# Whole turns of a cosine as int32 from ScalarE, in a planned kernel of attention and two gated layers

## The chip, the cores and the metric

One core of a Trainium2 chip runs the whole program. The metric is the device time of one execution in microseconds, the median over the runs. TensorE multiplies matrices, VectorE, ScalarE and GpSimd work on tiles in SBUF (VectorE and ScalarE also on the banks of PSUM that TensorE writes), and SyncE issues nearly all transfers. In the views PE is TensorE's matmul, PEld its load of weights, DVE is VectorE, ACT ScalarE, POOL GpSimd and SP SyncE.

## What is computed

```python
def _moe_ref(x, w_in, w_out):
    h = x @ w_in
    g = h * np.clip(h + 3.0, 0.0, 6.0) / 6.0
    return g @ w_out

def _moe2_ref(x, w_in, w_out):
    h = x @ w_in
    g = h * np.cos(h)
    return g @ w_out

def reference(q, k, v, moe, moe2):
    a = _attn_ref(q, k, v)           # (2, 8, 768, 64): local window and block summaries
    x = a.transpose(0, 2, 1, 3).reshape(1536, 512)
    return _moe2_ref(_moe_ref(x, *moe), *moe2)
```

Both layers take 1536 tokens of 512 features to 2048 and back; the weights arrive as float64 and are read as pairs of 32-bit words.

## The kernel before, in words

The program has three stages: attention, layer 1 (the clipped gate) and layer 2 (the cosine gate). Every matrix factor is held as two parts, a rounded one (hi) and the rest (lo), and a product is three matmuls, hi by hi, hi by lo and lo by hi. `unpack` (L693 to L709) rebuilds a float from each pair of words of a weight: a ScalarE step (L696) and two VectorE steps (L700, L704). `parts` then makes the two halves of a weight tile wi or wo: a copy (L445 on ScalarE, L447 on GpSimd) and a subtraction (L452, VectorE or GpSimd).

The tokens form three blocks of 512, the 2048 features 16 chunks of 128 in four groups. In layer 2 each group has two *stretches*, where two chunks of the first two blocks are computed together by a scheme with seven products in place of eight (`unit`, L957; `pairs`, L723, prepares sums of weights at L733). Its intermediate sums o and s are made on VectorE from bank t (L1002). The third block's chunks are computed singly (`g1`, L754, matmuls at L766 to L768). Second matmuls (`g2`, L823, matmuls at L842) fill in between, and their results are added to part or pc on VectorE (L883). PSUM has eight banks: two each named acc, h and s, one t and one o.

Behind each first matmul comes `post` (L772 to L823), which makes g and its two parts out of a bank h (or t, o, s). In layer 1 that is one ScalarE step into a tile n and one VectorE step into a tile r. In layer 2 the cosine is computed by taking off whole turns:

```python
act(ACTF.Identity, n, h, ..., scale=1.0 / (2.0 * math.pi), bias=bias[:, 1:2])   # + MAGIC
n = n - MAGIC                       # L810, GpSimd or VectorE
stt(-C1, r, n, h, ...)              # r = h - C1 n, first step, L802
stt(-C2, r, n, r, ...)              # r = r - C2 n, second step, L802
act(ACTF.Abs, r, r, ...)
act(ACTF.Sin, r, r, ..., scale=-1.0, bias=bias[:, 2:3])
r = r * h                           # L817
```

MAGIC is 1.5 times 2 to the 23, so that adding it in float32 rounds to whole numbers. Then come the copy of r into g (L445 or L447) and the subtraction r - g (L452). The bank is free once L817 has read it. All ScalarE steps of `post` stand at L798, all `scalar_tensor_tensor` steps at L802.

The order of all instructions is written by a planner in the program. `Plan.op` collects operations with their candidate engines, costs and priorities; `order` plays them through on a model of the engines and emits each where that model puts it. An operation marked `port=True` counts as excluding GpSimd while VectorE runs it. A table T holds offsets of priorities, loads of engines and numbers of buffers, and NUDGES a list of seeds that disturb priorities. A change of a cost, a mark or the tables therefore moves rows on every engine and in SyncE's queue of loads.

Of the kernel before, what the change touches and what calls it, by code (L numbers as in the profile page):

```python
# [12 lines left out]
F32 = mybir.dt.float32  # L13
F32R = mybir.dt.float32r
U32 = mybir.dt.uint32
ACTF = mybir.ActivationFunctionType
ALU = mybir.AluOpType
AX = mybir.AxisListType
# [22 lines left out]
AW = QD + 2 * (NS - 1)  # L41
SP = S + 2 * WIN
NEG = -8.0e9
MAGIC = 1.5 * 2.0 ** 23
C1 = 6.28125
C2 = 2.0 * math.pi - 6.28125

# [16 lines left out]
def consts():  # L64
# [11 lines left out]


T = dict(
    A0=-16.558, AS=2.479, mask=-41.168, kp=-24.799, lk=-15.792, lq=-45.051, lv=4.367, wl=4.037, wc=-16.709,
    g0=37.025, gi=15.494, pp=74.729, fill=0.951, DVE=1.408, POOL=0.57, d0=0.9, warm=9, tail=1, lagq=1, nraw=3,  # L80
    ncf=2, n=5, w1=5, n2=1, g2=5, w2=3, f2=1, ne=3, npt=2, nz=3, u0=10.0, us=-1.723, vpe=27.388, lvt=-27.618,
    avg=-15.727,
)
NUDGES = (
    301030, 301046, 301214, 301262, 301298, 301299, 301311, 301317, 301338, 301363, 301389, 301404, 301405,
    301511, 301663, 301665, 301951, 302350, 302504, 302970, 303048, 303239, 303835, 304073, 304314, 304762,
    304806, 306020, 401406, 404014, 1004772,
)


# [37 lines left out]
class Plan:  # L128
# [10 lines left out]
    def op(self, engs, fn, prio, r=(), w=(), take=(), port=False, mode=0):  # L139
        o = Op()  # L140
        o.engs, o.fn, o.prio, o.port, o.mode, o.seq = engs, fn, prio, port, mode, len(self.ops)
        o.wait, o.after, o.ready, o.takes = 0, [], 0.0, list(take)
        o.start = o.eng = None
        o.took = False
        bufs = {id(x): x for x in take}
        before = set()
        for key in r:
            before.add(self.writer[key])
        for key in w:
            if key in self.writer:  # L150
                before.add(self.writer[key])
            before.update(self.readers.get(key, ()))
        for key in r:
            self.readers.setdefault(key, []).append(o)
        for key in w:
            self.writer[key] = o
            self.readers[key] = []
        for key in (*r, *w):
            x = key[0] if isinstance(key, tuple) else key
            if isinstance(x, Buf):  # L160
                bufs[id(x)] = x
        o.uses = list(bufs.values())
        for x in o.uses:
            x.uses += 1
        for key in r:
            x = key[0] if isinstance(key, tuple) else key
            if isinstance(x, Buf) and x.cls.bank:
                for a in self.readers[key]:
                    if a is not o and not (len(engs) == 1 and list(a.engs) == list(engs)):
                        before.add(a)  # L170
        before.discard(o)
        for x in before:
            x.after.append(o)
        o.wait = len(before)
        self.ops.append(o)
        return o
# [217 lines left out]
def body(ctx: ExitStack, tc: tile.TileContext, q, k, v, vf, w_in1, w_out1, w_in2, w_out2, ident_d, mask_d, avg_d, out):  # L394
    nc = tc.nc
    w_in = (w_in1.bitcast(U32), w_in2.bitcast(U32))
    w_out = (w_out1.bitcast(U32), w_out2.bitcast(U32))
    cp = ctx.enter_context(tc.tile_pool(name="cp", bufs=1))
    pp = ctx.enter_context(tc.tile_pool(name="pp", bufs=1, space=bass.MemoryType.PSUM))
# [3 lines left out]
    def slots(name, n, shape, dtype=F32, fifo=True, pool=cp, later=0):  # L403
        return Slots(lambda i, pool=pool: pool.tile(shape, dtype, name=f"{name}{i}"), n, later, fifo, pool is pp)

    mask = ap.tile([P, 3, CE], F32, name="mask")
    bias = cp.tile([P, 4], F32, name="bias")
# [5 lines left out]
    avg = ap.tile([P, AW + QD], F32, name="avg")  # L413
# [9 lines left out]
    ident = ap.tile([P, P], F32, name="ident")  # L423
    c_raw = slots("raw", T["nraw"], [P, DM, 2], U32)
    c_cu = slots("cu", 2, [P, DM])
# [15 lines left out]
    eng = {"DVE": nc.vector, "POOL": nc.gpsimd}  # L441

    def copy(e, out, in_, scale=1.0):
        if e == "ACT":
            nc.scalar.activation(out=out, in_=in_, func=ACTF.Copy, scale=scale)  # L445
        elif e == "POOL" or scale != 1.0:
            eng[e].tensor_scalar(out=out, in0=in_, scalar1=scale, scalar2=0.0, op0=ALU.mult, op1=ALU.add)  # L447
        else:
            nc.vector.tensor_copy(out, in_)

    def sub(e, out, in0, in1):
        eng[e].tensor_tensor(out=out, in0=in0, in1=in1.bitcast(F32), op=ALU.subtract)  # L452
# [6 lines left out]
    for x in c_vs.tiles:  # L459
        nc.gpsimd.memset(x, 0.0)  # L460
    nc.vector.memset(bias[:, 0:1], 0.5)
    nc.vector.memset(bias[:, 1:2], MAGIC)
    nc.vector.memset(bias[:, 2:3], 0.5 * math.pi)
    pl = Plan()
    op = pl.op
    pl.second = [c_cf, c_wi, c_g, c_n, c_r, c_p2, c_sx]
# [149 lines left out]
    def soft(h, sp, c0, e_, sm, prio):  # L616
        for i in range(HT):
            t = HT * h + i
            mk = mask[:, 0 if t == 0 else (2 if t == TB - 1 else 1), :]
            for o in range(2):  # L620
# [11 lines left out]
                    lambda e, x=x: nc.scalar.activation(  # L632
                        out=e_.t[:, x, :], in_=e_.t[:, x, :], func=ACTF.Exp, scale=-1.0,
                        bias=sm.t[:, x:x + 1], accum_out=sm.t[:, N4 + x:N4 + x + 1],
# [21 lines left out]

    A0, AS = T["A0"], T["AS"]
    load_consts()
# [7 lines left out]
    for b, h, ps in units:  # L666
        pr = A0 + AS * HT * y
        if h == 0:
# [23 lines left out]
    def unpack(src, prio, f, key, take):  # L692
# [3 lines left out]
           lambda e: nc.scalar.activation(  # L696
               out=u.t, in_=raw.t.bitcast(F32)[:, :, 1], func=ACTF.Prelu, scale=2.0 ** -112, alpha=2.0 ** 32),
           prio, r=[raw], w=[u], take=[u])
        op({"DVE": 0.34},
           lambda e: eng[e].tensor_scalar(  # L700
               out=f().bitcast(U32), in0=raw.t[:, :, 0], scalar1=2.0 ** -29, scalar2=7.0, op0=ALU.mult, op1=ALU.min),
           prio, r=[raw], w=[key], take=take, port=True)
        op({"DVE": 0.602},
           lambda e: nc.vector.scalar_tensor_tensor(  # L704
               out=f().bitcast(U32), in0=u.t.bitcast(U32), scalar=3, in1=f().bitcast(U32),
               op0=ALU.logical_shift_left, op1=ALU.bitwise_or),
# [33 lines left out]
    IT = 5.2  # L740
    G0 = A0 + AS * HT * NP + T["g0"]

# [32 lines left out]
    def post(it, hb, pr):  # L775
        L, N = it[0], it[5] - it[4]
        nb, rb, gb = Buf(c_n), Buf(c_r), Buf(c_g)

        def t(fixed, per):
            return fixed + per * N / TOK  # L780

        def h():
            return hb.t[:, 0:N]

        def n():
            return nb.row[:, 0:N]

        def r():
            return rb.row[:, 0:N]

        def hi():
            return gb.t[:, 0, 0:N]

        def lo():
            return gb.t[:, 1, 0:N]

        def act(func, out, in_, pr, fixed, rd, wr, take=(), **kw):
            op({"ACT": t(fixed, 0.43)}, lambda e: nc.scalar.activation(out=out(), in_=in_(), func=func, **kw), pr,  # L798
               r=rd, w=wr, take=take)

        def stt(s, out, a, b, o0, o1, rd, take=()):
            op({"DVE": t(0.056, 0.542)}, lambda e: nc.vector.scalar_tensor_tensor(  # L802
                out=out(), in0=a(), scalar=s, in1=b(), op0=o0, op1=o1), pr, r=rd, w=[rb], take=take)

        if L == 0:
            act(ACTF.Relu, n, h, pr, 0.146, [hb], [nb], [nb], scale=1.0 / 6.0, bias=bias[:, 0:1])
            stt(1.0, r, n, h, ALU.min, ALU.mult, [nb, hb], [rb])
        else:
            act(ACTF.Identity, n, h, pr, 0.146, [hb], [nb], [nb], scale=1.0 / (2.0 * math.pi), bias=bias[:, 1:2])
            op({"POOL": t(0.12, 0.463), "DVE": t(0.07, 0.265)}, lambda e: eng[e].tensor_scalar(  # L810
                out=n(), in0=n(), scalar1=1.0, scalar2=-MAGIC, op0=ALU.mult, op1=ALU.add), pr, w=[nb],
                port=True)
            stt(-C1, r, n, h, ALU.mult, ALU.add, [nb, hb], [rb])
            stt(-C2, r, n, r, ALU.mult, ALU.add, [nb])
            act(ACTF.Abs, r, r, pr, 0.11, [], [rb])
            act(ACTF.Sin, r, r, pr, 0.2, [], [rb], scale=-1.0, bias=bias[:, 2:3])
            op({"DVE": t(0.056, 0.542)}, lambda e: nc.vector.tensor_tensor(out=r(), in0=r(), in1=h(), op=ALU.mult),  # L817
               pr, r=[hb], w=[rb])
        op({"ACT": t(0.09, 0.435), "POOL": t(0.12, 0.463)}, lambda e: copy(e, hi(), r()), pr, r=[rb], w=[(gb, 0)],
           take=[gb])  # L820
        op({"DVE": t(0.07, 0.54), "POOL": t(0.125, 1.13)}, lambda e: sub(e, lo(), r(), hi()), pr,
           r=[rb, (gb, 0)], w=[(gb, 1)], port=True)
        return gb  # L823
# [85 lines left out]
    n = 0  # L909
# [7 lines left out]
    for j in range(NBLK):  # L917
        for x, y in ((0, TOK // 2), (TOK // 2, TOK)) if j == 0 else ((0, TOK),):
# [4 lines left out]
            for c in range(GS):  # L923
                pr = vt(n1 + c * d)
# [9 lines left out]
    pr = vt(T["u0"] - T["us"])  # L934
# [158 lines left out]
```

## Time and profile before

| | |
|---|---|
| median of 3 runs | 615.54 us (614.97 to 617.27) |
| the profiled execution | 616.4 us, of which the span of its trace is 614.5 |
| TensorE busy | 575.4 us, 94% of the span |
| VectorE busy | 486.8 us, 79% |
| GpSimd busy | 419.8 us, 68% |
| ScalarE busy | 314.0 us, 51% |
| mean granted TensorE clock | 0.992 of 2.4 GHz |

Busy time counts an instruction from its start to its end, and so contains what it waits for another engine in between. A row for a group of instructions gives the count, the busy time and the mean, then the idle time of the engine just ahead of them and what ended it. A clock of 1.00 is 2.4 GHz, of 0.50 is 1.2 GHz. A table by stage gives the busy time of each engine in a stretch of the span.

### The profile page before, as it was taken

The numbers are of one execution on the slowest core, as the hardware profiler recorded it, in microseconds if no ns is written. First come the engines' busy times: TensorE is split into PE (matmuls) and PEld (weight loads), VectorE is DVE, ScalarE is ACT, GpSimd is POOL, SyncE is SP. The second block draws the span as 40 slices with busy tenths as digits, with TensorE's granted clock in tenths as the row PEclk, the third lists the DMA queues.
The fourth block names the chain that finished last, engine by engine and source line by source line (L and its number), as shares of the span: only waits on it lengthen the run. The fifth ranks groups of instructions, "written<-read, shape, count | busy, mean of one in ns | idle before, by whom it ended". The sixth has DMA issues, their size and how long they took to land. (4 is left out here: it accounts for less than half of the span.)

```text
span 614.5 us, 9208 instructions
## 1 busy us (share of the span) xinstructions
PE 575.4 (94%) x3308; PEld 465.7 (76%) x3308; DVE 486.8 (79%) x807; ACT 314.0 (51%) x657; POOL 419.8 (68%) x417
## 2 busy tenths in 40 slices
PE   5868999999999999999999899999898999989997
PEld 4657988877788888888886577877786787867786
DVE  3599877998888379836989989975998689986962
ACT  2799877456433233223345666564543546445430
POOL 2579755999785458645989867956677668946540
PEclk9999999999999999999999999998999999989999
DMA  9999820013224004400330203220114003200122
GB/s 224 279 297 275 243 70 2 1 35 105 80 99 162 1 2 129 146 0 1 103 103 0 69 1 103 74 99 0 69 34 141 32 1 103 69 0 0 40 76 92
DMA packets 28910, 51.62 MB, mean 84 GB/s; under 512 B 14529, under 2 KB 17985, under 8 KB 28865
## 3 DMA queue, kind: packets, MB, share of 16 engines
q1 hardware_dynamic: 28720, 50.97, 27.1%
q8 instruction: 26, 0.43, 0.3%
q14 instruction: 20, 0.16, 0.1%
q10 hardware_dynamic: 144, 0.07, 0.0%
HBM read 47.88 MB, written 3.15 MB: 83 GB/s over the span
## 5 line engine op out<-in xcount | busy, mean ns | idle before, releaser
L452 POOL TENSOR_TENSOR g<-r,g 128x512 fp32r<-128x512 f32 (+1 forms) x78 | 108.9, 1397 | 5.3 <-ACT g L445 1.3
L447 POOL TENSOR_SCALAR g<-r 128x512 fp32r<-128x512 f32 (+1 forms) x57 | 39.8, 698 | 72.1 <-DVE r L802 48.7
L842 PE MATMUL acc<-g,wo 128*128 128x512 f32 (+1 forms) x384 | 87.7, 366 | 1.3 <-DVE g L452 1.3
L696 ACT ACTIVATE cu<-raw 128x512 f32<-128x512 f32 x64 | 43.1, 674 | 78.2 <-DVE cf L704 61.4
L842 PEld LDWEIGHTS acc<-g,wo 128*128 128x128 f32 x384 | 66.2, 189 | 14.3 <-DVE g L452 2.1
L842 PE MATMUL acc<-wo,g 128*128 128x512 f32 x288 | 73.7, 390 | 0.6 <-DVE pc L883 0.6
L842 PE MATMUL s<-wo,g 128*128 128x512 f32 x288 | 72.9, 394 | 0.0
L842 PEld LDWEIGHTS s<-wo,g 128*128 128x128 f32 x288 | 55.1, 191 | 12.0 <-DVE pc L883 0.4
L842 PEld LDWEIGHTS acc<-wo,g 128*128 128x128 f32 x288 | 54.0, 188 | 12.6 <-DVE pc L883 1.1
L704 DVE SCALAR_TENSOR_TENSOR cf<-cu,cf 128x512 uint32<-128x512 uint32 x64 | 62.0, 979 | 0.6
L842 PE MATMUL s<-g,wo 128*128 128x512 f32 x240 | 59.0, 389 | 0.0
L452 POOL TENSOR_TENSOR wi<-cf,wi 128x512 fp32r<-128x512 f32 x37 | 57.0, 1544 | 1.4
L810 POOL TENSOR_SCALAR n<-n 128x512 f32<-128x512 f32 x40 | 31.9, 798 | 37.3 <-ACT n L798 37.3
L842 PEld LDWEIGHTS s<-g,wo 128*128 128x128 f32 x240 | 45.1, 188 | 9.4
L700 DVE TENSOR_SCALAR cf<-raw 128x512 uint32<-128x512 uint32 x64 | 49.7, 795 | 2.4 <-POOL wo L452 1.5
L994 PE MATMUL t<-sx,wi 128*128 128x512 f32 x168 | 45.8, 408 | 6.1 <-DVE o L1002 5.8
L798 ACT ACTIVATE r<-r 128x512 f32<-128x512 f32 x48 | 30.2, 631 | 41.4 <-DVE r L802 41.4
L798 ACT ACTIVATE n<-h,bias 128x512 f32<-128x512 f32 (+1 forms) x42 | 26.9, 641 | 38.6 <-PE h L994 29.7
L766 PE MATMUL h<-xh,wi 128*128 128x512 f32 (+1 forms) x112 | 42.9, 383 | 3.7 <-ACT n L445 2.9
L632 ACT ACTIVATE e<-e,sm 128x120 f32<-128x120 f32 x96 | 36.9, 388 | 16.9 <-DVE sm L624 15.7
L802 DVE SCALAR_TENSOR_TENSOR r<-n,r 128x512 f32<-128x512 f32 x48 | 45.0, 946 | 0.6
L994 PEld LDWEIGHTS t<-sx,wi 128*128 128x128 f32 x168 | 31.6, 193 | 16.6 <-DVE o L1002 8.8
(145 smaller groups left out, 1367.4 us busy)
## 6 DMA issues: line engine op xcount, KB each, us to landing
raw<-in_w_in_dram SPq DMA_DIRECT2D x32, 512.0 KB, 3.8
raw<-in_w_out_dram SPq DMA_DIRECT2D x32, 512.0 KB, 3.7
kw<-in_k_dram SPq DMA_DIRECT2D x8, 576.0 KB, 7.4
vw<-in_v_dram SPq DMA_DIRECT2D x8, 576.0 KB, 8.9
z<-in_q_dram SPq DMA_DIRECT2D x24, 128.0 KB, 4.7
out_dram<-part SPq DMA_DIRECT2D x8, 256.0 KB, 2.0
y<-in_vt_dram SPq DMA_DIRECT2D x4, 384.0 KB, 4.7
out_dram<-pc SPq DMA_DIRECT2D x3, 256.0 KB, 2.0
```

The source lines that it names most:

```text
L447: eng[e].tensor_scalar(out=out, in0=in_, scalar1=scale, scalar2=0.0, op0=ALU.mult, op1=ALU.add)
L452: eng[e].tensor_tensor(out=out, in0=in0, in1=in1.bitcast(F32), op=ALU.subtract)
L632: lambda e, x=x: nc.scalar.activation(out=e_.t[:, x, :], in_=e_.t[:, x, :], func=ACTF.Exp, scale=-1.0, bias=sm.t[:, x:x + 1], accum_out=sm ...
L696: lambda e: nc.scalar.activation(out=u.t, in_=raw.t.bitcast(F32)[:, :, 1], func=ACTF.Prelu, scale=2.0 ** -112, alpha=2.0 ** 32),
L700: lambda e: eng[e].tensor_scalar(out=f().bitcast(U32), in0=raw.t[:, :, 0], scalar1=2.0 ** -29, scalar2=7.0, op0=ALU.mult, op1=ALU.min),
L704: lambda e: nc.vector.scalar_tensor_tensor(out=f().bitcast(U32), in0=u.t.bitcast(U32), scalar=3, in1=f().bitcast(U32), op0=ALU.logical_shi ...
L766: nc.tensor.matmul(out=o, lhsT=wh, rhs=hi, start=(kk == 0), stop=False)
L798: op({"ACT": t(fixed, 0.43)}, lambda e: nc.scalar.activation(out=out(), in_=in_(), func=func, **kw), pr, r=rd, w=wr, take=take)
L802: op({"DVE": t(0.056, 0.542)}, lambda e: nc.vector.scalar_tensor_tensor(out=out(), in0=a(), scalar=s, in1=b(), op0=o0, op1=o1), pr, r=rd, ...
L810: op({"POOL": t(0.12, 0.463), "DVE": t(0.07, 0.265)}, lambda e: eng[e].tensor_scalar(out=n(), in0=n(), scalar1=1.0, scalar2=-MAGIC, op0=AL ...
L842: nc.tensor.matmul(out=o, lhsT=l, rhs=r, start=(c == 0 and z == 0), stop=(c == GS - 1 and z == 2))
L994: nc.tensor.matmul(out=bank.t, lhsT=stat(u), rhs=get(v), start=(first and q == z == 0), stop=(q == 1 and z == 2), skip_group_check=True)
```

## The change

In layer 2, ScalarE writes h / 2 pi into the tile n as int32, with a plain copy in place of the step that adds MAGIC, and the conversion leaves whole turns. The step at L810 goes, with the constant in the bias tile. The two reduction steps read n as int32. In `stt`, a step that doesn't read the bank (the second one) is marked as excluding GpSimd in the plan. T and NUDGES have new numbers. In the changed program the lines behind the first edits are one less, those of `post` other: the reduction steps are at L804, L817 is L816, L1002 is L1001, L700 and L704 are L699 and L703, and L733 is L732.

```diff
-MAGIC = 1.5 * 2.0 ** 23
...
-    A0=-16.558, AS=2.479, mask=-41.168, kp=-24.799, lk=-15.792, lq=-45.051, lv=4.367, wl=4.037, wc=-16.709,
+    A0=-13.801, AS=2.467, mask=-39.355, kp=-32.071, lk=-11.912, lq=-44.667, lv=2.333, wl=1.389, wc=-17.88,
...
-    nc.vector.memset(bias[:, 1:2], MAGIC)
-    nc.vector.memset(bias[:, 2:3], 0.5 * math.pi)
+    nc.vector.memset(bias[:, 1:2], 0.5 * math.pi)
...
+        def turns():
+            return n().bitcast(I32)
+
         def stt(s, out, a, b, o0, o1, rd, take=()):
             op({"DVE": t(0.056, 0.542)}, lambda e: nc.vector.scalar_tensor_tensor(
-                out=out(), in0=a(), scalar=s, in1=b(), op0=o0, op1=o1), pr, r=rd, w=[rb], take=take)
+                out=out(), in0=a(), scalar=s, in1=b(), op0=o0, op1=o1), pr, r=rd, w=[rb], take=take, port=hb not in rd)
...
-            act(ACTF.Identity, n, h, pr, 0.146, [hb], [nb], [nb], scale=1.0 / (2.0 * math.pi), bias=bias[:, 1:2])
-            op({"POOL": t(0.12, 0.463), "DVE": t(0.07, 0.265)}, lambda e: eng[e].tensor_scalar(
-                out=n(), in0=n(), scalar1=1.0, scalar2=-MAGIC, op0=ALU.mult, op1=ALU.add), pr, w=[nb],
-                port=True)
-            stt(-C1, r, n, h, ALU.mult, ALU.add, [nb, hb], [rb])
-            stt(-C2, r, n, r, ALU.mult, ALU.add, [nb])
+            act(ACTF.Copy, turns, h, pr, 0.146, [hb], [nb], [nb], scale=1.0 / (2.0 * math.pi))
+            stt(-C1, r, turns, h, ALU.mult, ALU.add, [nb, hb], [rb])
+            stt(-C2, r, turns, r, ALU.mult, ALU.add, [nb])
             act(ACTF.Abs, r, r, pr, 0.11, [], [rb])
-            act(ACTF.Sin, r, r, pr, 0.2, [], [rb], scale=-1.0, bias=bias[:, 2:3])
+            act(ACTF.Sin, r, r, pr, 0.2, [], [rb], scale=-1.0, bias=bias[:, 1:2])
```

Three places of the order follow. A row has its line, operation, what it writes and what it reads; the number behind a name is that of the buffer.

GpSimd in the first stretch of layer 2's second group (around 402 to 416 us of the trace), before:

```order
L452 TENSOR_TENSOR wi_118<-cf_115,wi_118 128x512
L810 TENSOR_SCALAR n_126<-n_126 128x512
L810 TENSOR_SCALAR n_1496<-n_1496 128x512
L810 TENSOR_SCALAR n_127<-n_127 128x512
L452 TENSOR_TENSOR g_1495<-r_129,g_1495 128x512
L810 TENSOR_SCALAR n_126<-n_126 128x512
L447 TENSOR_SCALAR g_130<-r_1497 128x512
L452 TENSOR_TENSOR g_130<-r_1497,g_130 128x512
L447 TENSOR_SCALAR g_131<-r_128 128x512
```

And in the changed program:

```order
L452 TENSOR_TENSOR wi_119<-cf_115,wi_119 128x512
L447 TENSOR_SCALAR g_1494<-r_129 128x512
L452 TENSOR_TENSOR g_1494<-r_129,g_1494 128x512
L447 TENSOR_SCALAR g_130<-r_128 128x512
L452 TENSOR_TENSOR g_130<-r_128,g_130 128x512
L447 TENSOR_SCALAR g_131<-r_1496 128x512
```

Between the last weights of the stretch and the wo that come next, GpSimd has copies and subtractions of g alone.

VectorE in the second stretch of the same group (around 427 to 438 us), ahead of the third block's single chunk that waits for bank t; before:

```order
L802 SCALAR_TENSOR_TENSOR r_128<-n_126,s_140 128x512
L817 TENSOR_TENSOR r_1497<-r_1497,h_136 128x512
L802 SCALAR_TENSOR_TENSOR r_128<-n_126,r_128 128x512
L810 TENSOR_SCALAR n_1496<-n_1496 128x512
L452 TENSOR_TENSOR wo_124<-cf_1487,wo_124 128x512
L802 SCALAR_TENSOR_TENSOR r_129<-n_1496,o_139 128x512
L802 SCALAR_TENSOR_TENSOR r_1497<-n_127,t_138 128x512
L817 TENSOR_TENSOR r_128<-r_128,s_140 128x512
L802 SCALAR_TENSOR_TENSOR r_1497<-n_127,r_1497 128x512
L802 SCALAR_TENSOR_TENSOR r_129<-n_1496,r_129 128x512
L700 TENSOR_SCALAR cf_114<-raw_109 128x512
L700 TENSOR_SCALAR cf_115<-raw_110 128x512
```

And in the changed program:

```order
L804 SCALAR_TENSOR_TENSOR r_1496<-n_127,s_140 128x512
L452 TENSOR_TENSOR wo_122<-cf_114,wo_122 128x512
L816 TENSOR_TENSOR r_128<-r_128,h_136 128x512
L804 SCALAR_TENSOR_TENSOR r_1496<-n_127,r_1496 128x512
L804 SCALAR_TENSOR_TENSOR r_129<-n_1495,o_139 128x512
L452 TENSOR_TENSOR wo_124<-cf_115,wo_124 128x512
L804 SCALAR_TENSOR_TENSOR r_128<-n_126,t_138 128x512
L804 SCALAR_TENSOR_TENSOR r_129<-n_1495,r_129 128x512
L804 SCALAR_TENSOR_TENSOR r_128<-n_126,r_128 128x512
L816 TENSOR_TENSOR r_1496<-r_1496,s_140 128x512
L699 TENSOR_SCALAR cf_114<-raw_109 128x512
L699 TENSOR_SCALAR cf_1486<-raw_110 128x512
```

The step n between the second step of s and wo_124 is gone, and the other steps keep their sequence but for small swaps.

SyncE's first loads (z is a piece of q, kw one of k with its window, vw one of v); before:

```order
L481 DMA z_83<-in_q_dram 128x256
L481 DMA z_84<-in_q_dram 128x256
L481 DMA z_85<-in_q_dram 128x256
L481 DMA mask<-in_mask_dram 128x120
L481 DMA kw_104<-in_k_dram 128x12x96
L481 DMA kw_105<-in_k_dram 128x12x96
L481 DMA kw_106<-in_k_dram 128x12x96
L481 DMA avg<-in_avg_dram 128x86
L481 DMA vw_86<-in_v_dram 96x1536
L481 DMA kw_107<-in_k_dram 128x12x96
L481 DMA z_83<-in_q_dram 128x256
L481 DMA vw_87<-in_v_dram 96x1536
```

And in the changed program:

```order
L480 DMA z_83<-in_q_dram 128x256
L480 DMA kw_104<-in_k_dram 128x12x96
L480 DMA z_84<-in_q_dram 128x256
L480 DMA z_85<-in_q_dram 128x256
L480 DMA mask<-in_mask_dram 128x120
L480 DMA avg<-in_avg_dram 128x86
L480 DMA kw_105<-in_k_dram 128x12x96
L480 DMA vw_86<-in_v_dram 96x1536
L480 DMA kw_106<-in_k_dram 128x12x96
L480 DMA vw_87<-in_v_dram 96x1536
L480 DMA z_83<-in_q_dram 128x256
L480 DMA kw_107<-in_k_dram 128x12x96
```

The loads of k and v alternate now, with the first k three places further up and the third and fourth two places further down; in both programs the first weights follow as the eighteenth load.

## Rows read from the trace of the kernel before

**Rows 1.** Busy time of each engine, with its share of the span.

```profile
PE 575.4 (94%) x3308; PEld 465.7 (76%) x3308; DVE 486.8 (79%) x807; ACT 314.0 (51%) x657; POOL 419.8 (68%) x417
```

**Rows 2.** Busy time by stage: PE, PEld, DVE, ACT, POOL, PEclk, DMA share, GB/s.

```profile
0.00:60.00 60.00, 43.18 (x641) 33.88 (x642) 41.93 (x174) 43.04 (x153) 37.24 (x57) 1.00 1.01 272
...
180.00:300.00 120.00, 120.00 (x531) 99.41 (x530) 84.18 (x109) 38.60 (x61) 72.42 (x69) 1.00 0.20 66
300.00:580.00 280.00, 262.89 (x1109) 209.35 (x1108) 242.31 (x306) 151.02 (x246) 205.91 (x192) 0.98 0.16 51
```

**Rows 3.** TensorE's waits, 300 to 580 us: total, times, longest.

```profile
PE t L994 <- DVE o L1002: 5.8, 4, 2.6
PE t L766 <- DVE r L817: 5.0, 4, 1.9
PE h L766 <- ACT n L445: 2.9, 3, 2.0
```

**Rows 4.** By stage: stretches under full clock (a third, 540 to 550, has 0.83).

```profile
415.00:420.00 5.00, 3.71 (x9) 2.93 (x10) 1.29 (x2) 1.79 (x4) 4.20 (x5) 0.66 0.00 0
470.00:480.00 10.00, 7.44 (x26) 5.66 (x25) 8.54 (x13) 4.45 (x7) 3.08 (x4) 0.83 0.51 160
```

**Rows 5.** Groups of instructions: count, busy us, mean ns, idle ahead.

```profile
L810 POOL TENSOR_SCALAR n<-n 128x512 f32<-128x512 f32 x40 | 31.9, 798 | 37.3 <-ACT n L798 37.3
L802 DVE SCALAR_TENSOR_TENSOR r<-n,r 128x512 f32<-128x512 f32 x48 | 45.0, 946 | 0.6
```

**Rows 6.** Lines L810, L802 and L700: least, median and longest ns.

```profile
L810 POOL TENSOR_SCALAR n<-n x40: 611/624/1167, 333.2 to 589.8; 128x512 f32<-128x512 f32 x40
L810 DVE TENSOR_SCALAR n<-n x8: 426/914/1518, 342.6 to 587.1; 128x512 f32<-128x512 f32 x8
L802 DVE SCALAR_TENSOR_TENSOR r<-n,r x48: 675/693/1806, 336.6 to 591.2; 128x512 f32<-128x512 f32 x48
L802 DVE SCALAR_TENSOR_TENSOR r<-n,t x22: 672/675/689, 127.8 to 582.6; 128x512 f32<-128x512 f32 x22
L700 DVE TENSOR_SCALAR cf<-raw x64: 408/832/1724, 28.6 to 540.3; 128x512 uint32<-128x512 uint32 x64
```

**Rows 7.** ScalarE steps of lines L798 and L445, the same columns.

```profile
L798 ACT ACTIVATE n<-h,bias x42: 454/680/712, 44.1 to 586.3; 128x512 f32<-128x512 f32 x34, 128x256 f32<-128x256 f32 x8
L445 ACT ACTIVATE n<-h x14: 577/582/601, 133.8 to 556.0; 128x512 f32<-128x512 f32 x14
L798 ACT ACTIVATE r<-r,bias x48: 705/722/729, 339.2 to 592.6; 128x512 f32<-128x512 f32 x48
```

**Rows 8.** Groups of instructions on GpSimd.

```profile
L452 POOL TENSOR_TENSOR wi<-cf,wi 128x512 fp32r<-128x512 f32 x37 | 57.0, 1544 | 1.4
L447 POOL TENSOR_SCALAR g<-r 128x512 fp32r<-128x512 f32 (+1 forms) x57 | 39.8, 698 | 72.1 <-DVE r L802 48.7 <-DVE r L817 21.2 <-PE s L842 0.8
```

**Rows 9.** Timeline ahead of 438.50 us: start, duration, engine; in brackets the idle time.

```profile
430.12 1.51 DVE L810 TENSOR_SCALAR n<-n 128x512 f32<-128x512 f32 x1
...
436.02 1.84 DVE L700 TENSOR_SCALAR cf<-raw 128x512 uint32<-128x512 uint32 x2
...
438.50 0.50 PE L766 MATMUL t<-xh,wi 128*128 128x512 f32 x1 [1.92 <-DVE r L817]
```

**Rows 10.** Timeline ahead of 416.29 us.

```profile
409.52 0.62 POOL L810 TENSOR_SCALAR n<-n 128x512 f32<-128x512 f32 x1 [2.49 <-ACT n L798]
...
410.89 1.51 DVE L802 SCALAR_TENSOR_TENSOR r<-n,r 128x512 f32<-128x512 f32 x1
...
416.29 0.72 PE L766 MATMUL h<-xh,wi 128*128 128x512 f32 x1 [1.96 <-ACT n L445]
```

**Rows 11.** Timeline ahead of 473.32 us.

```profile
470.56 1.75 DVE L452 TENSOR_TENSOR wi<-cf,wi 128x512 fp32r<-128x512 f32 x1
...
473.32 0.97 PE L994 MATMUL t<-sx,wi 128*128 128x512 f32 x3 [2.56 <-DVE o L1002]
```

**Rows 12.** Transfers by line: KB each, median us from issue to landing.

```profile
kw<-in_k_dram SPq DMA_DIRECT2D x8, 576.0 KB, 7.4
```

More of the change, by code (lines that the diff above doesn't have):

```diff
@@ L15 @@
 U32 = mybir.dt.uint32
+I32 = mybir.dt.int32
 ACTF = mybir.ActivationFunctionType
@@ L78 @@
 T = dict(
-    A0=-16.558, AS=2.479, mask=-41.168, kp=-24.799, lk=-15.792, lq=-45.051, lv=4.367, wl=4.037, wc=-16.709,
-    g0=37.025, gi=15.494, pp=74.729, fill=0.951, DVE=1.408, POOL=0.57, d0=0.9, warm=9, tail=1, lagq=1, nraw=3,
-    ncf=2, n=5, w1=5, n2=1, g2=5, w2=3, f2=1, ne=3, npt=2, nz=3, u0=10.0, us=-1.723, vpe=27.388, lvt=-27.618,
-    avg=-15.727,
+    A0=-13.801, AS=2.467, mask=-39.355, kp=-32.071, lk=-11.912, lq=-44.667, lv=2.333, wl=1.389, wc=-17.88,
+    g0=37.96, gi=14.518, pp=83.365, fill=-4.275, DVE=1.431, POOL=0.686, d0=0.9, warm=9, tail=1, lagq=1, nraw=3,
+    ncf=2, n=5, w1=5, n2=1, g2=5, w2=3, f2=1, ne=3, npt=2, nz=3, u0=10.0, us=3.653, vpe=22.852, lvt=-24.759,
+    avg=-18.65,
 )
 NUDGES = (
-    301030, 301046, 301214, 301262, 301298, 301299, 301311, 301317, 301338, 301363, 301389, 301404, 301405,
-    301511, 301663, 301665, 301951, 302350, 302504, 302970, 303048, 303239, 303835, 304073, 304314, 304762,
-    304806, 306020, 401406, 404014, 1004772,
+    1013, 1040, 1044, 1279, 1395, 2050, 2075, 2161, 2222, 2527, 2663, 2677, 2796, 2985, 3178, 3288, 4056, 4936,
+    8127, 8135, 8202, 8206, 8216, 8235, 8284, 8325, 8376, 8407, 501307, 502568, 502984, 503132, 503483, 503838,
+    505142, 505219, 505582, 506608, 507425,
 )
```

## The prediction

> **What bounds the kernel now.** I read the busy totals first. TensorE is busy for 575.4 of 614.5 us [rows 1], so a gain can come only from the 39.1 us in which it isn't, and from stretches at its lower clock. The table by stage says where they lie [rows 2]: 16.8 us in the first 60 (60 - 43.18), which the loads set (the DMA share is 1.01); nothing from 180 to 300; 17.1 us from 300 to 580 (280 - 262.89); the other 5.2 us are spread over 60 to 180 and the tail. The stretch from 300 to 580 is layer 2, the only layer with the cosine, and in it VectorE is busy for 242.3 of 280 us and GpSimd for 205.9. From 180 to 300, in layer 1, the same kind of matmuls runs without an idle microsecond while those two engines are busy for 84.2 and 72.4 of 120. So in layer 2 the side work is what TensorE waits for.
>
> Next, the list of TensorE's waits in that stretch [rows 3]. Three kinds make 13.7 of the 17.1 us: a product in bank t waits for the sum o (L1002), which still reads t; a single chunk in t waits until the cosine's last product (L817) has read it; h waits for a copy on ScalarE that stands behind a cosine. After three of these waits TensorE runs for a while at 1.2 instead of 2.4 GHz [rows 4]: a mean clock of 0.66 over 5 us, and twice 0.83 over 10 us, costs at most 1.7 + 1.7 + 1.7 = 5.1 us. **Layer 2 thus has 17.1 + 5.1 = 22.2 us to give back**, and no more.
>
> **The change, part by part.** *The step that goes.* L810 runs 48 times: 40 times on GpSimd at a mean of 798 ns, 31.9 us [rows 5], and 8 times on VectorE at a median of 914 ns, some 7.3 us [rows 6]. Undisturbed it takes 611 and 426 ns; what is over that is waiting for the other engine. The second reduction step r<-n,r takes 675 ns at best, 946 in the mean and 1806 at worst [rows 5, 6], while the first step, which reads its bank in PSUM, stays between 672 and 689 [rows 6]. So the second step does wait for GpSimd: 48 x (946 - 675) = 13 us of VectorE's busy time are such waits. The plan of before did not count that step among those that exclude GpSimd, the new one does; by itself that costs nothing, it moves the order.
>
> *The chain of one cosine.* A bank stays taken from its matmuls to L817. Between stood the ScalarE step, L810, two VectorE steps, two ScalarE steps and L817. Without L810 that is at least 0.61 us shorter, or 0.43 where VectorE had it, plus what it waited in the queues.
>
> *The ScalarE step* becomes a plain copy of a PSUM bank with a scale and no bias tile. The form with bias has a median of 680 ns, a plain copy of h into an n tile 582 [rows 7]: 0.10 us less in each chain. Writing int32 is not in the trace; the bounds are 0.58 (that copy) and 0.72 us (the longest ScalarE step of this size), and I take 0.58, since source and width are those of that copy. Plain copies stand between the sines already, so I expect no table to be loaded anew. VectorE now reads int32. Its L700 on uint32 operands takes 408 ns at best against 426 for L810 on f32 [rows 6], so I take no difference; bounds 0 and 14 ns for each of the 96 steps (689 - 675, the spread of the undisturbed first step), 1.3 us.
>
> *What the plan moves.* The matmuls stay the same in number. GpSimd is filled again: 8 more full copies g (60 for 52) at 0.698 us and 5 more subtractions wi (42 for 37) at 1.544 [rows 8], 5.6 + 7.7 = 13.3 us, so of its 31.9 us some 18.6 come free. VectorE gives up these 5 wi and its 8 steps n, and takes 4 more full subtractions g (25 for 21). In the first stretch of the second group, GpSimd had three steps n in a row between weights and copies g; in its second stretch an n on VectorE stood ahead of a wo and four steps r. Both places are shown with the change.
>
> *The sum, wait by wait.* (a) t waits for L817, 5.0 us. The instance at 438.50, 1.92 us long, is typical: VectorE's rows ahead of it follow one another without a gap and hold a step n of 1.51 us, and two L700 of 1.84 together for 0.82 [rows 6, 9]. The n alone is worth 1.51 of the 1.92. I take 4.0 of 5.0 (bounds 1.5, one such n, and 5.0). (b) h waits for ScalarE, 2.9 us. At 416.29 the chain goes back to an n on GpSimd at 409.52 and a second step of 1.51 us, 0.83 over its best [rows 6, 10]: 0.62 + 0.10 + 0.83 are at stake. I take 2.0 (bounds 0.7, the n and the shorter copy once, and 2.9), and half of the 1.7 us of low clock behind it, 0.8. (c) t waits for the sum o, 5.8 us. Here the preparation of weights stands ahead: at 473.32 it is a subtraction wi of 1.75 us on VectorE [rows 11]. The change helps only by emptying the queues earlier. I take a third, 2.0 (bounds 0 and 5.8), and a third of the 3.4 us of low clock behind two of them, 1.2. (d) Of the other 3.4 us, most of it where layer 1 turns into layer 2, I take 0.5 (bounds 0 and 3.4). (e) The opening and layer 1 are planned anew, with the same work: 0, with bounds of plus and minus 2.1 us, one k load of 576 KB moved in a stream of 272 GB/s [rows 2, 12]. The same seventeen loads stand ahead of the first weights in both programs.
>
> Sum: 4.0 + 2.8 + 3.2 + 0.5 = 10.5 us. The profiled execution took 616.4 us (its span of 614.5 and 1.9 around it), so 605.9 there. It stands 0.9 above the median of 615.54, so **605.0 us** is the forecast.
>
> The Trainium skill (SBUF — State Buffer, section "Who interferes with whom") says that a VectorE instruction with two SBUF inputs contends with a GpSimd instruction that reads SBUF, and (section "SBUF: two separate sides") that whichever starts first keeps the other out for its whole length. The second step's 1806 ns, 1.1 us over its best [rows 6], agree with that. By this rule int32 leaves the second step as exclusive as it was, and the subtractions that stay on GpSimd hold it off as before: by it alone the sum loses (a) and (c) and is that of the first rival, against 10.5 us by the rows of (a) to (d).
>
> **The rivals.**
> 1. *The exclusion eats the gain.* The subtractions wi, 1.54 us each in the mean [rows 8], hold VectorE off where n did, GpSimd is filled again by 13.3 us, and (a) and (c) stay. For it: n is shorter than those subtractions. Against: VectorE loses its own 7.3 us of n for good. Then 2.8 + 0.5 = 3.3 us are won: 612.2 us.
> 2. *The opening comes later (slower).* The third k load moves from the seventh place of the queue to the ninth, behind avg and the first v; taken as one load of the size of k, that is 2.1 us at 272 GB/s [rows 2, 12], and the fourth goes two places down as well. As TensorE has no idle time from 180 to 300, a delay of the opening reaches the end in full. At twice 2.1 us it decides once layer 2 gives back under 1.1 us: with 0.5 us won there, 615.5 + 4.2 - 0.5 = 619.2 us. Against: the first k load comes up three places, and the loads ahead of the weights are the same.
> 3. *Nearly all of it goes.* VectorE gets ahead of TensorE as in layer 1, and 18 of the 22.2 us go: 597.5 us. For it: layer 1 shows none of these waits. Against: (c) hangs on weights, not on cosines.
> 4. *The int32 write is slow*, say twice 0.58 us. ScalarE has room (151.0 of 280 us, [rows 2]), but the chain gets no shorter; (b) goes and half of (a), 4.8 us: 615.5 - 5.7 = 609.8 us. No row speaks for it.
>
> **How the numbers follow.** Forecast 0.59, with 601 to 610.5 as its own range; rival 1 0.17, rival 2 0.09, rival 3 0.10, rival 4 0.05. The range from 598 to 616 holds the forecast, rivals 1 and 4 and about half of rival 3, and leaves out rival 2 and the rest, 0.15 to 0.2. A measurement of this kernel tells 0.5% (3.1 us) from no change, so the bounds are 612.5 and 618.6. Faster: the forecast, rivals 3 and 4, and the cases of rival 1 with luck in (e), 0.78. The same: most of rival 1 and the milder cases of rival 2, 0.14. Slower: 0.08.
>
> **What would show it.** Right: r<-n,r nearer to 675 in the mean; the copy into n at some 0.58 us; GpSimd near 400 us; TensorE idle for under 11 us from 300 to 580, the wait of t for L817 almost gone and that for L1002 the largest left; fewer stretches under full clock. Wrong: r<-n,r still above 0.9 with the waits for L817 at 4 us or more (rival 1); more than 20 us idle in the first 60 (rival 2); a copy into n over 1 us (rival 4).

## The result, and the profile after

The changed kernel takes 600.45 us (median of 4 runs, 597.58 to 601.13) against 615.28 for the kernel before: a ratio of 0.9743, 95% interval 0.9706 to 0.9781. It is 14.8 us faster; 10.5 were forecast. The profiled execution took 601.13 us.

Busy time of each engine, changed kernel (before: [rows 1]):

```profile
PE 569.4 (95%) x3308; PEld 465.0 (78%) x3308; DVE 470.9 (79%) x799; ACT 305.1 (51%) x648; POOL 396.0 (66%) x385
```

Busy time by stage (the columns of [rows 2]):

```profile
0.00:60.00 60.00, 42.95 (x599) 34.18 (x600) 40.08 (x167) 38.83 (x139) 32.92 (x51) 0.80 0.99 261
...
180.00:300.00 120.00, 120.00 (x531) 99.38 (x530) 83.85 (x107) 38.70 (x62) 70.71 (x68) 1.00 0.21 66
300.00:565.00 265.00, 257.99 (x1121) 208.64 (x1120) 234.03 (x301) 145.34 (x242) 192.97 (x169) 1.00 0.17 55
```

In layer 2 TensorE is idle for 7.0 us instead of 17.1, and its clock is full throughout, where it lost up to 5.1 us before. The opening is no better (17.1 us idle in the first 60 against 16.8) and ran at a mean clock of 0.80. TensorE's waits from 300 to 565 us (before: [rows 3]):

```profile
PE t L993 <- DVE o L1001: 2.7, 3, 1.1
PE acc L841 <- DVE g L452: 1.2, 1, 1.2
PE h L766 <- DVE xl L452: 0.8, 1, 0.8
PE h L993 <- DVE r L804: 0.7, 1, 0.7
PE t L993 <- ACT t L445: 0.5, 1, 0.5
PE h L765 <- ACT n L445: 0.5, 1, 0.5
```

The wait of a single chunk in t for the cosine's last product (L817 before, L816 now) was 5.0 us and isn't in the list any more. That for the sum o fell from 5.8 to 2.7, that of h for the copy on ScalarE from 2.9 to 0.5. The three instances of [rows 9 to 11], on the timeline of the changed kernel:

```profile
415.67 0.50 PE L765 MATMUL h<-xh,wi 128*128 128x512 f32 x1 [0.47 <-ACT n L445]
...
433.55 0.50 PE L765 MATMUL t<-xh,wi 128*128 128x512 f32 x1
...
467.15 1.67 PE L993 MATMUL t<-sx,wi 128*128 128x512 f32 x6 [1.02 <-DVE o L1001]
```

The 1.96 us of [rows 10] became 0.47, the 1.92 of [rows 9] too little to be listed, the 2.56 of [rows 11] 1.02. Now the steps themselves, by the lines of the changed kernel (least, median and longest ns; before: [rows 6, 7]):

```profile
L797 ACT ACTIVATE n<-h x16: 577/597/600, 334.0 to 571.1; 128x512 int32<-128x512 f32 x16
...
L804 DVE SCALAR_TENSOR_TENSOR r<-n,r x48: 678/747/1783, 337.4 to 575.8; 128x512 f32<-128x512 int32 x48
...
L804 DVE SCALAR_TENSOR_TENSOR r<-n,t x22: 673/676/689, 128.1 to 564.9; 128x512 f32<-128x512 int32 x12, 128x512 f32<-128x512 f32 x10
```

The int32 write takes 597 ns. The reading of int32 costs nothing: the first step of bank t has a mean of 677 ns on int32 and of 679 on float32. But the second step still waits for GpSimd: as a group its mean is 972 ns, where it was 946 [rows 5]:

```profile
L804 DVE SCALAR_TENSOR_TENSOR r<-n,r 128x512 f32<-128x512 int32 x48 | 46.3, 972 | 0.4
```

To set layer 2 apart from the opening I counted matmuls in the traces (3308 in each, the first with number 0) and took the starts of number 1146, still in attention, of number 2200, in layer 2's first stretch, and of the last. "Layer 2" in the table is the time between the latter two, in the one execution of each kernel that was profiled.

| kernel | median us | 1146th | 2200th | last | layer 2 |
|---|---|---|---|---|---|
| before | 615.28 | 100.95 | 333.37 | 610.34 | 276.97 |
| changed | 600.45 | 103.11 | 335.95 | 595.19 | 259.24 |
| changed, measured again | 598.52 | 97.62 | 330.45 | 589.63 | 259.18 |

So layer 2 gave 17.7 us, the same in two executions of the changed kernel, while the opening came out 2.2 us later in one and 3.3 us earlier in the other.

### The profile page after: what moved, and what is told of

Same layout as the page of the kernel before. It is cut to its first block, busy times and chain, and to the rows that moved or that the text cites. A ratio compares the mean times of both kernels' runs of the same rounds, so it can differ in the third digit from the quotient of the medians.

```text
span 599.4 us, 9179 instructions
## 1 busy us (share of the span) xinstructions
PE 569.4 (95%) x3308; PEld 465.0 (78%) x3308; DVE 470.9 (79%) x799; ACT 305.1 (51%) x648; POOL 396.0 (66%) x385
## 4 chain that ended last, share of the span: by engine, by line
PE 61%; DVE 21%; POOL 5%; issue 4%; ACT 4%; DMA 4%; SPq 0%; DVEq 0%; POOLq 0%; ACTq 0%
PE acc L841 15%; PE s L841 14%; PE t L993 7%; PE h L993 5%; DVE r L804 4%; DVE cf L699 3%; PE h L765 3%; PE h L766 3%; PE h L767 3%; DVE g L452 3%; PE o L993 2%; DVE cf L703 2%; PE o L597 2%; DMA z<-in_q_dram 2%; PE t L586 1%
## 5 line engine op out<-in xcount | busy, mean ns | idle before, releaser
L447 POOL TENSOR_SCALAR g<-r 128x512 fp32r<-128x512 f32 (+1 forms) x64 | 48.3, 755 | 99.7 <-DVE r L816 49.7
L452 POOL TENSOR_TENSOR g<-r,g 128x512 fp32r<-128x512 f32 (+1 forms) x72 | 100.4, 1397 | 3.9
L841 PEld LDWEIGHTS acc<-g,wo 128*128 128x128 f32 x384 | 66.0, 189 | 14.8 <-DVE g L452 3.6
L841 PE MATMUL s<-wo,g 128*128 128x512 f32 x288 | 71.0, 389 | 0.0
L452 POOL TENSOR_TENSOR wi<-cf,wi 128x512 fp32r<-128x512 f32 x42 | 64.0, 1530 | 3.5 <-ACT wi L445 2.4
L703 DVE SCALAR_TENSOR_TENSOR cf<-cu,cf 128x512 uint32<-128x512 uint32 x64 | 56.4, 896 | 0.3
L699 DVE TENSOR_SCALAR cf<-raw 128x512 uint32<-128x512 uint32 x64 | 50.2, 802 | 1.6 <-POOL wo L452 1.5
L993 PE MATMUL t<-sx,wi 128*128 128x512 f32 x168 | 44.1, 397 | 3.5 <-DVE o L1001 2.9
L804 DVE SCALAR_TENSOR_TENSOR r<-n,r 128x512 f32<-128x512 int32 x48 | 46.3, 972 | 0.4
L765 PE MATMUL h<-xh,wi 128*128 128x512 f32 (+1 forms) x112 | 43.1, 385 | 1.1 <-ACT wi L445 0.6
L766 PE MATMUL h<-xl,wi 128*128 128x512 f32 (+1 forms) x112 | 40.9, 366 | 1.0 <-DVE xl L452 0.8
L767 PE MATMUL h<-xh,wi 128*128 128x512 f32 (+1 forms) x112 | 40.8, 365 | 0.9 <-POOL wi L452 0.9
L993 PE MATMUL h<-xh,wi 128*128 128x512 f32 x112 | 41.2, 389 | 0.0
```

The lines of the kernel that those rows point to most:

```text
L699: lambda e: eng[e].tensor_scalar(out=f().bitcast(U32), in0=raw.t[:, :, 0], scalar1=2.0 ** -29, scalar2=7.0, op0=ALU.mult, op1=ALU.min),
L703: lambda e: nc.vector.scalar_tensor_tensor(out=f().bitcast(U32), in0=u.t.bitcast(U32), scalar=3, in1=f().bitcast(U32), op0=ALU.logical_shi ...
L765: nc.tensor.matmul(out=o, lhsT=wh, rhs=hi, start=(kk == 0), stop=False)
L766: nc.tensor.matmul(out=o, lhsT=wh, rhs=lo, start=False, stop=False)
L767: nc.tensor.matmul(out=o, lhsT=wl, rhs=hi, start=False, stop=(kk == KT - 1))
L841: nc.tensor.matmul(out=o, lhsT=l, rhs=r, start=(c == 0 and z == 0), stop=(c == GS - 1 and z == 2))
```

## The experiments

The planner makes a new order whenever a cost or a step changes, so an edit and its order can't be told apart by editing alone. In most runs the planner therefore got the operations of one kernel, and only what an operation emits was changed: the order and the engines stay as they were, row for row. Theory A: the step itself made the gain. Theory B: the newly searched order did.

**Old order, steps out.**

```diff
-            act(ACTF.Identity, n, h, pr, ..., bias=bias[:, 1:2])
+            act(ACTF.Copy, turns, h, pr, ...)
             op({"POOL": t(0.12, 0.463), "DVE": t(0.07, 0.265)},
-               lambda e: eng[e].tensor_scalar(out=n(), in0=n(), ..., scalar2=-MAGIC, ...), pr, w=[nb], port=True)
+               lambda e: None, pr, w=[nb], port=True)
-            stt(-C1, r, n, h, ...), stt(-C2, r, n, r, ...)
+            stt(-C1, r, turns, h, ...), stt(-C2, r, turns, r, ...)
```

> The order and the engines of before, row for row, with the 48 steps n (L810) taken out and the whole turns written as int32 by a plain copy. Theory A, the step itself (its time on GpSimd and VectorE, and its place in the chain) is what layer 2 won: 603 to 607 us, the waits of t for L817 under 2 us. Theory B, the newly searched order is: 611 to 614 us, the waits for L817 still at 3 us or more.

603.77 us, ratio 0.9819 (0.9779 to 0.9860); layer 2 took 264.84 us, 12.1 less than before. TensorE's waits from 300 us on:

```profile
PE t L996 <- DVE o L1004: 3.5, 3, 1.7
PE h L767 <- ACT n L446: 2.4, 2, 2.1
...
PE t L767 <- DVE r L819: 0.6, 1, 0.6
```

This is theory A. Without any new order the waits for the last product fell from 5.0 to 0.6 us and two thirds of layer 2's gain are there. The wait of h for the copy on ScalarE stayed (2.4 for 2.9), against my term (b).

**The same with the bias kept on ScalarE** (`Identity` with a bias tile of zeros, writing int32).

> As the first run, but ScalarE keeps the form with a bias tile (zeros in it), 0.68 in place of 0.60 us. Theory A: within 1 us of the first run, since ScalarE has room. Rival C, the shorter ScalarE step shortens the chain that decides: 3 us or more above the first run.

604.62 us, ratio 0.9848 (0.9807 to 0.9890); layer 2 263.62 us. The shorter ScalarE step isn't seen.

**Out of the chain, but still a load.** In each place of a step n now stands a step on a tile that nobody else uses (the lines are against the first run).

```diff
+    spare = cp.tile([P, 432], F32, name="spare")
...
-               lambda e: None, pr, w=[nb], port=True)
+               lambda e: eng[e].tensor_scalar(out=spare, in0=spare, scalar1=1.0, scalar2=0.0, ...), pr, w=[nb], port=True)
```

> As the first run, but each step n is replaced on its engine, in its place, by a step of the same kind on a spare tile of 432 columns that nobody waits for: out of the chain, still a load on GpSimd and VectorE. If the chain's length decides: within 2 us of the first run. If the time on the two engines and their mutual exclusion decides: 611 to 615 us, near before.

614.12 us, ratio 0.9981 (0.9947 to 1.0015); layer 2 273.71 us. The shorter chain gives at most 3.3 us of layer 2's 12.1 (276.97 - 273.71); a part of that may be the load's, which is narrower than before (432 columns for 512). The load gives the rest.

**New order, steps back.** The changed kernel's order with rounding by the constant, all 48 steps on GpSimd, each right behind its ScalarE step.

```diff
-            act(ACTF.Copy, turns, h, pr, ...)
+            def whole(e):
+                nc.scalar.activation(out=n(), in_=h(), func=ACTF.Identity, ..., bias=bias[:, 2:3])
+                nc.gpsimd.tensor_scalar(out=n(), in0=n(), scalar1=1.0, scalar2=-MAGIC, ...)
+            op({"ACT": t(0.146, 0.43)}, whole, pr, r=[hb], w=[nb], take=[nb])
```

> The order of the changed kernel, row for row, with rounding by the constant put back: ScalarE with bias, a step n on GpSimd right behind each of the 48, float reduction steps. Theory A: 610 to 618 us, most of the gain lost. Theory B: at most 604 us.

628.22 us, ratio 1.0218 (1.0160 to 1.0275); layer 2 288.12 us. That is 10 us beyond what I had expected of theory A: this order has no room for the steps. It mixes their price with that of places which no plan chose for them, so it doesn't measure the step by itself. Its waits, on the same view:

```profile
PE h L767 <- ACT n L446: 8.9, 3, 3.6
PE t L999 <- ACT t L446: 4.0, 4, 1.7
PE t L999 <- DVE o L1007: 3.5, 4, 1.6
PE t L767 <- DVE r L822: 2.7, 2, 1.9
```

**What of the load counts.** Next I kept the load on GpSimd alone, once as a step that reads and writes the spare tile, once as a fill that only writes it, and then as two fills in each place (against the run with the load kept).

```diff
-               lambda e: eng[e].tensor_scalar(out=spare, in0=spare, ...)
+               lambda e: eng[e].tensor_scalar(out=spare, in0=spare, ...) if e == "POOL" else None      # reading step
+               lambda e: nc.gpsimd.memset(spare, 1.0) if e == "POOL" else None                         # fill
+               lambda e: [nc.gpsimd.memset(spare, 1.0) for _ in range(2)] if e == "POOL" else None     # two fills
```

Reading step:

> As the run with the load kept, but only the 40 steps on GpSimd stand there (a step on a spare tile of 432 columns, reading and writing SBUF); the 8 on VectorE are gone. If GpSimd's share of the load decides: 609 to 614 us. If the 8 steps on VectorE did most of it: 604 to 607 us.

Fill:

> As the run just before, but each of the 40 steps on GpSimd is a fill of the spare tile, which writes SBUF and reads nothing. If it is GpSimd's own time that decides: within 2 us of the run just before, with allowance for a shorter step. If it is that a reading GpSimd step keeps VectorE's two-input steps out: near the run with the steps taken out, 603 to 606 us.

Two fills:

> As the run with a fill on GpSimd, but two fills in each of the 40 places, some 0.93 us in place of 0.47, more than the 0.76 us in the mean of the reading step it stands for. If it is reading that matters: 605 to 608 us, still well under the reading step's 612.3. If GpSimd's time matters: 611 us or more.

And the base of these runs, with the tile in memory and nothing in the places:

> The old order with the steps out and nothing in their places, but with the spare tile in memory, as all runs with a load have it: the right base for them. Their layer 1 ended 1.5 us later than without the tile, so 604.5 to 606 us; if that delay came from the load, 603.8 us as without the tile.

| in GpSimd's 40 places | median us | ratio, 95% | layer 2 | GpSimd's mean |
|---|---|---|---|---|
| nothing, tile in memory | 606.18 | 0.9837 (0.9786 to 0.9889) | 263.81 | |
| fill | 606.24 | 0.9851 (0.9796 to 0.9906) | 264.40 | 474 ns |
| two fills | 607.17 | 0.9862 (0.9817 to 0.9906) | 266.10 | 2 x 470 ns |
| reading step | 612.31 | 0.9966 (0.9936 to 0.9996) | 274.73 | 753 ns |

By stage, 300 to 570 us (the columns of [rows 2]), with nothing in the places:

```profile
300.00:570.00 270.00, 261.95 (x1125) 209.55 (x1124) 236.69 (x303) 148.24 (x249) 179.18 (x156) 1.00 0.16 53
```

With the two fills:

```profile
300.00:570.00 270.00, 261.64 (x1115) 208.69 (x1114) 235.22 (x302) 147.01 (x246) 211.73 (x233) 0.99 0.16 53
```

With the reading step:

```profile
300.00:570.00 270.00, 257.44 (x1077) 204.97 (x1076) 235.12 (x290) 143.40 (x240) 200.82 (x188) 0.97 0.16 53
```

And its own instructions, least, median and longest ns:

```profile
L816 POOL TENSOR_SCALAR spare<-spare x40: 543/604/1082, 334.7 to 588.6; 128x432 f32<-128x432 f32 x40
```

VectorE's second step of `unpack`, which like the second reduction step has both inputs in SBUF, from 330 to 580 us; with one fill, then with the reading step:

```profile
L707 DVE SCALAR_TENSOR_TENSOR cf<-cu,cf 128x512 uint32<-128x512 uint32 x26 | 22.6, 877 | 0.2
...
L707 DVE SCALAR_TENSOR_TENSOR cf<-cu,cf 128x512 uint32<-128x512 uint32 x26 | 26.1, 1014 | 0.2
```

In these 270 us two fills keep GpSimd busy for 11 us more than the reading step does (211.7 and 200.8), and yet TensorE gets through 1115 matmuls there against 1077. So GpSimd's time was nearly free: 0.6 us of layer 2 for one fill and 2.3 for two. **In the profiles the reading step cost 10.9 us of layer 2** (274.73 - 263.81), 8.6 more than two fills (274.73 - 266.10). In the medians it is less: 6.1 us above nothing and 5.1 above two fills. The profiled execution of the reading step, 615.51 us, was the slowest of its ten, and no trace shows a faster one. Of the 10.9 us, 4.5 are idle time of TensorE in the stretch (270 - 257.44 against 270 - 261.95), and most of the rest is low clock (0.97 against 1.00).

The traces show what the step does to VectorE. Of the 74 steps of layer 2 that are a second reduction step or a second step of `unpack`, 26 take over 0.8 us with nothing in the places, 25 with one fill, 21 with two and 36 with the reading step. Each of these ends 0.53 to 0.56 us behind the end of a step on GpSimd: nine of the 36 behind the reading step, none behind a fill. The fills aren't quite free for VectorE: the first step of `unpack` has a mean of 803 ns with nothing, 861 with one fill and 868 with two. A step that differs from a fill in its reading alone was not tried. The Trainium skill (SBUF — State Buffer, section "Who interferes with whom") says that a VectorE instruction with two SBUF inputs contends with a GpSimd instruction that reads SBUF and not with one that only writes it. These four runs agree with it.

**The plan made anew, not searched.** The changed kernel with T and NUDGES of before, with the mark on the second step and without.

```diff
-    A0=-13.801, AS=2.467, mask=-39.355, ...
+    A0=-16.558, AS=2.479, mask=-41.168, ...
...
-                out=out(), in0=a(), scalar=s, in1=b(), op0=o0, op1=o1), pr, r=rd, w=[rb], take=take, port=hb not in rd)
+                out=out(), in0=a(), scalar=s, in1=b(), op0=o0, op1=o1), pr, r=rd, w=[rb], take=take)
```

(The second pair of lines is in the run without the mark alone.)

> The changed kernel with T and NUDGES of before, so that the plan is made anew for the new steps, but not searched for them; the second step is marked. Theory B in its smaller form (what is left of the gain beside the step, some 3 to 6 us, is the search of the tables): 602 to 607 us, no better than the old order with the step out. If the mark or the plan's mere knowledge that n is gone gives it: 599 to 601 us.

605.87 us, ratio 0.9846 (0.9793 to 0.9899); layer 2 266.66 us. That is no better than the old order with the steps out (264.84).

> As the run just before, without the mark on the second step. If the mark is worth something in the plan: 2 us or more slower than the run just before. If not: within 2 us of it.

610.15 us, ratio 0.9908 (0.9878 to 0.9937); layer 2 269.26 us. The plan with the mark is 2.6 us better in layer 2. This is one pair of plans: another search might hide or widen it. With the old tables and the mark layer 2 is 7.5 us behind the changed kernel (266.66 - 259.18), so the searched tables are worth about that for this set of steps.

**The opening.** The changed kernel again, and with matmuls on zeros in a wait of the opening:

```diff
+            if not warmed:
+                warmed.append(1)
+                for _ in range(12):
+                    nc.tensor.matmul(out=c_h.tiles[0][:, 0:P], lhsT=idle[:, 0:P], rhs=idle[:, 0:P], start=True, stop=True)
```

> The changed kernel once more, to see its opening. Theory D, the opening's 2.2 us against before are not the new order of loads but a lower granted clock in the first 60 us of that one execution (0.80): where the clock is higher now, the 1146th matmul starts at 100 to 101 us as in the run of this order with the step put back (100.45 us at 0.94); where it is 0.80 again, near 103. Theory E, the order of loads: near 103 us whatever the clock.

598.52 us, ratio 0.9718 (0.9694 to 0.9742).

> The changed kernel with 12 more matmuls on zeros of 128 columns right behind the first scores, where TensorE waits 5.2 us for the second k. Theory D: the clock in the first 60 us at 0.95 or more, 597 to 599.5 us, a smaller spread. Theory E or no effect of the filling: within 0.5 us of the changed kernel; if the fill runs past the arrival of the second k: 1 to 2 us slower.

598.28 us, ratio 0.9729 (0.9701 to 0.9758), within 0.3 us of the same kernel without them. The first 60 us by stage, the changed kernel again:

```profile
0.00:60.00 60.00, 48.92 (x665) 39.54 (x666) 45.33 (x182) 43.84 (x153) 36.94 (x57) 0.91 1.01 283
```

With the matmuls on zeros:

```profile
0.00:60.00 60.00, 49.30 (x674) 40.60 (x675) 43.86 (x177) 42.31 (x150) 35.37 (x55) 0.86 0.99 273
```

Theory E falls: the same order of loads put matmul 1146 at 103.11, 97.62 and (steps put back) 100.45 us. Before it was at 100.95, and the eight profiles with that order, this one among them, have 100.78 to 102.92. Theory D is not shown either. The clock differs with it (0.80, 0.91, 0.94), but 0.91 gave the earliest opening, and the filling did not hold the clock at 0.95. What differs as well is when the second load of k is through. GpSimd's copy of its sums starts, in the changed kernel's first profile, at

```profile
12.67 0.43 POOL L447 TENSOR_SCALAR kw<-ks 128x288 f32<-128x288 f32 x1 [4.74 <-DVE ks L549]
```

and in the second, of the same program, at

```profile
10.32 0.43 POOL L447 TENSOR_SCALAR kw<-ks 128x288 f32<-128x288 f32 x1 [2.45 <-DVE ks L549]
```

Which comes first, late loads or the low clock, stays open; it is a difference between executions, not one of the change. No run is clearly faster than the changed kernel.

## Why the prediction was right

The range (598 to 616) and the sign held; the size was 4.5 us short, and 600.45 stands just under the forecast's own range (601 to 610.5). That it is no further off is in part luck: in layer 2 alone 17.7 us came for 10.5, and in the profiled execution the opening took 2.2 of them back. By its steps:

*Where the time was.* Right. All of the gain is in layer 2, where TensorE waits for side work: 17.7 us by the count of matmuls. The ceiling of 22.2 us was too low, though. It took idle time and clock alone. Counted from start to start, the matmuls from 320 to 580 us lost some 29 us before against a full rate of 0.227 us each, and 11 in the changed kernel. A matmul takes some 0.39 us though the next one starts after 0.227, and behind a wait the first takes longer still (at 438.50 us 0.50 [rows 9]); neither counts as idle time. Of the 17.7 us, 10.1 are idle time (17.1 - 7.0), up to 5.1 low clock, and the rest, some 2.5, was in no term of the sum.

*(a) t waits for L817*, 4.0 of 5.0 forecast: 5.0 came. With the old order and the steps out 4.4 of them did.

*(b) h waits for ScalarE*, 2.0 of 2.9: 2.4 came, but I can't lay it to the shorter chain, as I had put it. With the steps out of the old order only 0.5 of it went, and ScalarE's 0.10 us didn't count (layer 2 took 263.62 us without it against 264.84 with it). The rest came with the new order.

*(c) t waits for o*, 2.0 of 5.8: 3.1 came, 2.3 of it with the old order. That the queues ahead of it emptied earlier fits this; no run tried it by itself.

*The low clock*, 0.8 + 1.2 of 5.1 (a third of 3.4 is 1.1, not 1.2): all of it went. This is the term that was most undersized. I took shares of the low clock in the same measure as of the waits before it; but the waits that stayed are shorter, 1.2 us at most where the longest was 2.6, and the clock from 300 to 565 us is 1.00.

*(d)*, 0.5 of 3.4: nothing came, 3.8 us of other waits stay (7.0 - 2.7 - 0.5).

*(e) The opening*: 0 within 2.1 us. It was 2.2 us later in one profile and 3.3 us earlier in another, which the order of loads doesn't explain. Both lie outside the bounds: they took one load for all that can move there, and the same program varies by more.

*The second step.* I expected its mean nearer to 675 ns, as a sign that (a) is right. It went to 972. The sign was wrong though the term was right. In the changed kernel 24 of its 48 instances take over 0.8 us, and each of them ends 0.53 to 0.55 us behind the end of a step on GpSimd, twelve times of a subtraction g or wi, as rival 1 said. Rival 1's mechanism is real and did not eat the gain: VectorE had 8 steps less to run and 40 steps on GpSimd less to stand against. The relief shows at another step with two inputs in SBUF, the second one of `unpack` (330 to 580 us, before and changed):

```profile
L704 DVE SCALAR_TENSOR_TENSOR cf<-cu,cf 128x512 uint32<-128x512 uint32 x26 | 23.9, 929 | 0.2
...
L703 DVE SCALAR_TENSOR_TENSOR cf<-cu,cf 128x512 uint32<-128x512 uint32 x26 | 20.4, 800 | 0.1
```

The other signs came: the copy into n at 0.60 us, GpSimd at 396 us, 7.0 us of idle time, the wait for L1002 the largest left, no stretch of layer 2 under full clock.

*The price of the step.* The prediction named three: GpSimd's 31.9 us, VectorE's 7.3 and the chain's 0.61 us each. The runs order them: its removal gives 12.1 us in the old order, and a reading step back on GpSimd takes 10.9 of it away (in the medians 6.1), though it is out of the chain and narrower than the step n (432 columns for 512). The 8 steps on VectorE add nothing to that: layer 2 takes 273.71 us with them and 274.73 without. GpSimd's time by itself is worth 0.6 to 2.3, and the chain at most 3.3 when tried without the others; the parts overlap.

*Rivals 2 to 4.* The opening's order of loads is not slower; some 18 us went in layer 2, near rival 3, of which 14.8 showed in the median; the int32 write took 0.60 us.

## What to carry to other kernels

Where VectorE and GpSimd share the work, count a GpSimd step that reads SBUF as time of both: here 40 such steps cost 10.9 us in the profile and 6.1 in the median, while one or two fills in their places cost 0.6 and 2.3 (in the medians 0.1 and 1.0). To see what an edit does when a planner sets the order, hold the order fixed and change only what is emitted: that split 17.7 us into 12.1 for the step and the rest for the new order. And compare stages, not whole times, when the opening of a kernel varies by some us from one execution to the next.

## What the runs showed of the hardware that was not expected

A float tile of 432 columns that is only filled once at the start slowed layer 1: the 500 matmuls from number 1600 to 2100 took 114.88 us with it and 113.33 without, in the runs with nothing, a reading step or a fill alike, with TensorE busy all the time. It moves the tiles behind it by 1728 bytes; why that matters to TensorE was not tried.

The same program's opening varied by 5.5 us between two profiled executions (97.62 and 103.11 us at matmul 1146), while the time of its layer 2 agreed within 0.1 us.
